# A recurrent attention and a channel mix: value scaling and token differences of the later blocks move from VectorE to GpSimd

## The chip, the cores and the metric

The kernel runs on one core of a Trainium2 chip. The metric is the device time of one execution in microseconds (us), given as the median of several runs. The engines are named as in the profile: PE is TensorE (PEld its weight loads), DVE is VectorE, ACT is ScalarE, POOL is GpSimd, SP is SyncE. SP computes nothing here; it issues DMAs.

## The reference

A retention recurrence over 768 tokens for 4 batches and 8 heads of 64 channels, followed by a channel mix with two projections and a gate. Cut to the core:

```python
# q, k, v: (4, 8, 768, 64)
gamma = 1.0 - 2.0 ** (-5.0 - np.arange(H))
for t in range(S):
    state = gamma[None, :, None, None] * state + einsum('bhd,bhe->bhde', k[:, :, t], v[:, :, t])
    y[:, :, t] = scale * einsum('bhd,bhde->bhe', q[:, :, t], state)
x = y.transpose(0, 2, 1, 3).reshape(B, S, H * D)         # (4, 768, 512)
x_prev = concatenate([zeros, x[:, :-1, :]], axis=1)
xk = mu_k * x + (1.0 - mu_k) * x_prev
xr = mu_r * x + (1.0 - mu_r) * x_prev
k = maximum(xk @ w_k, 0.0)                               # 512 -> 1024
v = k * k @ w_v                                          # 1024 -> 512
out = 1.0 / (1.0 + exp(-(xr @ w_r))) * v
```

## The kernel before

The work is cut into twelve blocks of 256 tokens, three for each batch (block n is third n % 3 of batch n // 3). The recurrence is computed block by block as matmuls of scores, a masked intra-block part and a carried state; the channel mix of a block then uses the block's output, channels on partitions.

The order of all work is written out by hand in one long string, `ORDER` (lines 31 to 82). Each word is a step, its block, and after `~` the engine that runs it or issues its DMA (`p` GpSimd, `s` SyncE, `v` VectorE, `a` ScalarE). After `@` stand PSUM banks. Every engine executes its own steps in the order in which they stand in the string, and a step waits for what it needs; nothing reorders them.

The steps that matter here, with n the block:

- `lv.n`, `lq.n`, `lk.n` (`load`, lines 242 to 261): load values, queries and keys. Most of these are two DMAs each, one for every half of the tokens. Queries and keys are cast to fp16 on the way; values stay fp32. Values, queries and keys have four buffers each, so `lv.10` overwrites the values of block 6 and must wait until `vs.6` has read them.
- `vs.n` (`scale_v`, line 280): multiplies the values of a block (128 x 1024, fp32) with powers of gamma and writes fp16. Three buffers.
- `tq.n`, `tk.n` (line 351): for blocks 9, 10 and 11 alone, the queries and keys are transposed by a DMA on SyncE's queue, in the order tq.10, tk.10, tk.9, tq.9, tq.11, tk.11, with the stores of results (`st`, line 713) between them on the same queue. For the other blocks TensorE transposes (`Tq`, `Tk`).
- `S.n` (line 375): scores of a block on TensorE; `M.n` (line 420): mask, on VectorE.
- `C.n` (line 432 for blocks 6 to 11): the block's state from keys and scaled values, on TensorE. `U`, `G` (lines 485, 494): sum and decay of the state.
- `I.n`, `Y.n` (lines 507, 528): the block's output on TensorE, from the carried state and from the scaled values.
- `D.n` (`yout`, line 573 for blocks 6 to 11): moves the output from PSUM to the tile `xT` with its scale, on VectorE.
- `dx.n` (`differ`, line 595): difference of neighbouring tokens of `xT` (128 x 1024, fp32), for the mix.
- `X.n` (`mixed`, line 621): `dx * mu + x_prev` on VectorE, into `xk` and `xr`.
- `K` (lines 635, 645), `R` (688), `V` (700): the projections on TensorE. `O` (706): the result, on VectorE.

Blocks are grouped for the mix (`GROUPS`, line 19): blocks 6 and 7 form one group and 9 and 10 another, so the mix of block 6 is done with that of block 7.

Of the kernel before, what the change touches and what calls it, by code (L numbers as in the profile page):

```python
# [49 lines left out]
S.5.0@01 O.1.0 O.0.1 lv.5~p lq.6~p M.5.0~v S.5.1@23 vs.5~v K.3.2@5 Qa.3.3 lk.6~p Qb.3.3 K.3.5@4  # L50
M.5.1~v X.2.1.0 Qa.3.2 X.2.1.2 Tq.6@67 Qa.3.5 Tk.6@01 Eq.6~a lv.6~p lv.7~p Ek.6~a C.5@5 U.5.0
X.3.1.0 Qb.3.1 K.3.0@4 Qa.3.0 lk.7~p K.3.7@6 S.6@23 Qb.3.2 M.6~v I.5@01 Y.5 vs.6~v V.2.1.0@7
R.2.1@2 lv.10~p Qb.2.2 Qa.3.7 K.3.4@6 st.0.0 vs.7~v Qb.3.7 s.2.1 st.0.1 V.2.1.1 Tk.7@45 Qb.3.5
Qa.3.4 X.3.1.3 X.3.1.1 Qb.3.0 C.6@23 st.1.0 J.5 Ek.7~a X.3.1.2 R.2.0@6 lv.8~p U.6.0~a D.5~v
U.6.1 U.6.2 U.6.3 V.2.0.0@4 s.2.0 K.3.6@6 dx.5~v Qa.3.6 lq.8~p lk.8~p st.1.1 R.4.1@5 I.6@01
O.2.1 st.2.1 X.5.0.1 s.4.1 G.6~a V.2.0.1 O.2.0 X.5.1.0 X.5.0.3 R.3.1@6 s.3.1 C.7@23 U.7.0 S.7@45
Y.6 M.7~v V.3.1.0@7 X.5.0.2 D.6~v R.4.0@6 lk.9~p Qb.3.4 vs.8~v V.3.0.0@4 R.3.0@5 X.5.1.2 s.4.0
Qb.3.6 V.4.1.0@6 V.3.0.1 V.3.1.1 X.5.1.3 V.4.1.1 U.7.1 U.7.2 X.5.1.1 I.7@01 U.7.3 Tk.8@23 O.3.1
s.3.0 O.3.0 R.5.1@7 Ek.8~a st.3.1 lv.9~p dx.6~v X.5.0.0 s.5.1 C.8@45 Tq.8@23 Y.7 K.5.0@7 O.4.1
vs.9~v st.4.1 Eq.8~a D.7~v K.5.3@6 dx.7~v X.6.0.2 G.7~v Qa.5.0 Qb.5.0 st.2.0 lq.10~p tq.10~s  # L60
K.5.1@7 Qa.5.1 X.6.0.3 X.6.0.1 Qa.5.3 K.5.2@2 Qa.5.2 st.3.0 lk.10~p tk.10~s lv.11~p U.8.0 U.8.1
U.8.2 R.5.0@7 tk.9~s s.5.0 X.6.0.0 V.4.0.0@6 V.4.0.1 O.4.0 Qb.5.1 lk.11~p lq.9~p Qb.5.3
V.5.0.0@7 V.5.1.0@2 S.8@01 M.8~v I.8@45 X.6.1.3 Qb.5.2 V.5.0.1 K.6.4@6 X.6.1.1 O.5.0 Qa.6.4
K.6.7@3 Qa.6.7 K.6.3@6 Qa.6.3 X.6.1.0 lq.11~p X.6.1.2 K.6.1@3 Qa.6.1 Y.8 D.8~v C.9@01 Qb.6.1
vs.10~v U.9.0~a S.10@67 M.10~v U.9.1 dx.8~v X.8.0.3 X.8.0.2 Qb.6.3 K.6.6@3 X.8.0.0 Qb.6.7 Qa.6.6
Qb.6.6 V.5.1.1 K.6.2@4 Qa.6.2 X.8.0.1 Qb.6.2 K.6.5@3 tq.9~s Qa.6.5 R.6.1@4 s.6.1 tq.11~s st.5.0
K.6.0@6 O.5.1 U.9.2 U.9.3 G.9~v R.6.0@7 s.6.0 R.7.1@4 Qb.6.4 s.7.1 st.5.1 K.8.3@7 Qa.8.3 S.9@23
tk.11~s I.9@45 Qa.6.0 Qb.6.0 Qb.6.5 C.10@01 U.10.0 M.9~v R.7.0@7 s.7.0 U.10.1 U.10.2 U.10.3
K.8.2@6 K.8.1@2 Qa.8.1 vs.11~v Qb.8.1 V.6.0.0@7 Y.9 I.10@01 C.11@23 G.10~v V.6.0.1 Qa.8.2
V.7.1.0@6 D.9~v K.8.0@4 Qa.8.0 Qb.8.0 Qb.8.2 U.11.0 U.11.1 U.11.2 V.7.1.1 dx.9~v O.7.1 st.7.1  # L70
Qb.8.3 I.11@23 Y.10 D.10~v dx.10~v X.9.0.0 S.11@45 M.11~v X.9.0.2 V.7.0.0@6 V.7.0.1 V.6.1.0@0
V.6.1.1 V.8.0.0@1 V.8.0.1 X.9.0.1 V.8.1.0@4 V.8.1.1 st.4.0 X.9.0.3 K.9.0@5 O.7.0 K.9.4@6 X.9.1.1
Qa.9.0 Qa.9.4 Qb.9.4 X.9.1.0 O.6.0 st.6.0 Qb.9.0 X.9.1.3 X.8.1.2 Y.11 X.9.1.2 O.6.1 K.9.2@5
Qa.9.2 Qb.9.2 K.9.6@6 Qa.9.6 X.8.1.3 K.9.7@7 Qa.9.7 Qb.9.7 K.9.1@0 Qa.9.1 Qb.9.1 K.9.3@5 Qa.9.3
Qb.9.3 R.10.0@7 R.9.1@0 s.9.1 st.6.1 D.11~v R.9.0@5 s.9.0 st.7.0 X.8.1.1 K.9.5@6 V.10.1.0@5
Qa.9.5 Qb.9.5 Qb.9.6 V.10.0.0@6 X.8.1.0 dx.11~v R.8.1@0 s.8.1 V.9.1.0@2 R.8.0@0 X.11.0.2
X.11.1.3 X.11.0.0 X.11.0.3 X.11.0.1 K.11.1@3 s.8.0 K.11.3@0 Qa.11.3 O.8.0 st.8.0 s.10.0
V.9.0.0@1 Qa.11.1 Qb.11.1 K.11.2@0 Qa.11.2 O.8.1 st.8.1 K.11.0@7 X.11.1.2 V.10.0.1 Qb.11.2
Qb.11.3 V.9.1.1 Qa.11.0 R.10.1@0 Qb.11.0 V.10.1.1 O.9.1 st.9.1 s.10.1 X.11.1.0 X.11.1.1 V.9.0.1
# [794 lines left out]
```

## Time and profile before

| | |
|---|---|
| median of 3 runs | 154.39 us (154.21 to 154.42) |
| span of the profiled execution | 152.4 us, first to last instruction; the profile gives no other time of its own |
| PE busy | 145.3 us (95%) |
| DVE busy | 128.0 us (84%) |
| ACT busy | 94.5 us (62%) |
| POOL busy | 62.1 us (41%), all but four memsets of it DMA issues |
| granted TensorE clock | 1.000 over the whole span |

Times in the profile are counted from the start of the span. A row of a timeline gives the start, the length, the engine, the source line, the operation and tiles, and in brackets the idle time ahead of it and what ended that. In a row of DMA issues the last number is the time from issue to landing.

### The profile page before, as it was taken

The numbers are of one execution on the slowest core, as the hardware profiler recorded it, in microseconds if no ns is written. First come the engines' busy times: TensorE is split into PE (matmuls) and PEld (weight loads), VectorE is DVE, ScalarE is ACT, GpSimd is POOL, SyncE is SP. The second block draws the span as 40 slices with busy tenths as digits, with TensorE's granted clock in tenths as the row PEclk, the third lists the DMA queues.
The fourth block names the chain that finished last, engine by engine and source line by source line (L and its number), as shares of the span: only waits on it lengthen the run. The fifth ranks groups of instructions, "written<-read, shape, count | busy, mean of one in ns | idle before, by whom it ended". The sixth has DMA issues, their size and how long they took to land.

```text
span 152.4 us, 4956 instructions
## 1 busy us (share of the span) xinstructions
PE 145.3 (95%) x2129; PEld 82.4 (54%) x2129; DVE 128.0 (84%) x204; ACT 94.5 (62%) x172; POOL 62.1 (41%) x77
## 2 busy tenths in 40 slices
PE   7969899999999999999999999999999999999991
PEld 3345467657864545545448544447664444466460
DVE  2289999999999999999999998998999999331651
ACT  3655259979955679966418807869450089739430
POOL 7965658999746920599989000000000000000000
PEclk9999999999999999999999999999999999999999
DMA  5999999999999999299999999928103013003153
GB/s 146 237 241 192 181 240 237 148 148 223 167 178 216 213 225 286 68 239 166 258 188 238 236 168 126 152 89 109 38 4 138 0 71 142 0 0 138 69 207 138
DMA packets 56525, 23.83 MB, mean 156 GB/s; under 512 B 48056, under 2 KB 52024, under 8 KB 56504
## 3 DMA queue, kind: packets, MB, share of 16 engines
q0 software_dynamic: 45200, 14.95, 82.1%
q1 hardware_dynamic: 10872, 8.26, 22.3%
q8 instruction: 16, 0.26, 0.7%
q10 hardware_dynamic: 432, 0.32, 0.7%
q14 instruction: 5, 0.04, 0.1%
HBM read 24.31 MB, written 6.29 MB: 201 GB/s over the span
## 4 chain that ended last, share of the span: by engine, by line
PE 73%; DVE 11%; DMA 11%; issue 2%; ACT 0%; DVEq 0%; POOLq 0%
PE ps L700 24%; PE ps L688 14%; PE ps L635 12%; PE ps L645 11%; DMA kT<-k 6%; DMA v<-in_v_dram 5%; DVE a L420 3%; PE ps L507 2%; PE ps L311 2%; DVE xk L621 2%; DVE xT L580 2%; DVE dx L595 2%; PE ps L544 1%; DVE vs L280 1%; PE ps L388 1%
## 5 line engine op out<-in xcount | busy, mean ns | idle before, releaser
L700 PE MATMUL ps<-wv,k2s 128*128 128x512 f16 x184 | 43.9, 380 | 0.0
L667 ACT ACTIVATE kr<-ps 128x512 f32<-128x512 f32 x48 | 27.9, 594 | 23.0 <-PE ps L635 14.9
L700 PEld LDWEIGHTS <-k2s 128*128 128x128 f16 x184 | 17.2, 98 | 19.0
L706 DVE SCALAR_TENSOR_TENSOR os<-ps,rs 128x512 f32<-128x512 f32 x23 | 15.2, 684 | 12.1 <-PE ps L700 6.5
L688 PE MATMUL ps<-wr,xr 128*128 128x512 f16 x96 | 24.0, 379 | 0.0
L259 POOL DMA_DIRECT2D v<-in_v_dram x20 | 18.0, 911 | 13.6 <-DVE vs L280 8.3
L645 PE MATMUL ps<-xk,wk 128*128 128x256 f16 x192 | 23.4, 273 | 0.0
L635 PE MATMUL ps<-xk,wk 128*128 128x512 f16 x96 | 22.8, 379 | 0.0
L420 DVE TENSOR_TENSOR a<-ps,c_sb 128x1024 f16<-128x1024 f32 (+1 forms) x20 | 21.9, 1110 | 0.0
L694 ACT ACTIVATE rs<-ps 128x512 f32<-128x512 f32 x24 | 14.3, 594 | 10.6 <-PE ps L688 8.8
L645 PEld LDWEIGHTS <-wk 128*128 128x128 f16 x192 | 18.2, 98 | 3.9
L621 DVE SCALAR_TENSOR_TENSOR xr<-dx,mu,xT 128x256 f16<-128x256 f32 (+1 forms) x36 | 19.3, 566 | 0.0
L621 DVE SCALAR_TENSOR_TENSOR xk<-dx,mu,xT 128x256 f16<-128x256 f32 (+1 forms) x36 | 18.9, 569 | 0.3
L259 POOL DMA_DIRECT2D k<-in_k_dram x20 | 17.7, 896 | 3.5 <-DMA wv<-in_moe_w_v_dram 1.6
L280 DVE TENSOR_TENSOR vs<-v,csm_sb 128x1024 f16<-128x1024 f32 x12 | 14.5, 1217 | 3.3 <-DMA v<-in_v_dram 3.3
L675 ACT ACTIVATE k2s<-kr 128x512 f16<-128x512 f32 x24 | 14.7, 626 | 0.4
L595 DVE TENSOR_TENSOR dx<-xT 128x1024 f32<-128x1024 f32 x12 | 14.6, 1221 | 0.2
L635 PEld LDWEIGHTS <-wk 128*128 128x128 f16 x96 | 9.1, 98 | 10.5 <-issue 0.2
L679 ACT ACTIVATE k2s<-kr 128x512 f16<-128x512 f32 x24 | 14.5, 625 | 0.3
L688 PEld LDWEIGHTS <-xr 128*128 128x128 f16 x96 | 9.0, 98 | 10.0
L265 ACT COPY qT<-ps 128x1024 f16<-128x1024 f16 (+1 forms) x10 | 9.2, 924 | 7.7 <-PE ps L317 3.7
L265 ACT COPY kT<-ps 128x1024 f16<-128x1024 f16 (+1 forms) x10 | 9.3, 934 | 6.9 <-PE ps L306 3.4
(73 smaller groups left out, 151.3 us busy)
## 6 DMA issues: line engine op xcount, KB each, us to landing
out_dram<-os SPq DMA_DIRECT2D x23, 256.0 KB, 3.8
v<-in_v_dram POOLq DMA_DIRECT2D x20, 256.0 KB, 6.8
k<-in_k_dram POOLq DMA_DIRECT2D x21, 128.0 KB, 6.9
q<-in_q_dram POOLq DMA_DIRECT2D x13, 128.0 KB, 7.1
q<-in_q_dram POOLq DMA_DIRECT2D x5, 256.0 KB, 9.0
v<-in_v_dram POOLq DMA_DIRECT2D x2, 512.0 KB, 7.3
wv<-in_moe_w_v_dram POOLq DMA_DIRECT2D x2, 512.0 KB, 9.5
wk<-in_moe_w_k_dram POOLq DMA_DIRECT2D x2, 256.0 KB, 9.6
```

Of the source, the lines that this page charges most:

```text
L259: e.dma_start(out=to[:, i, hs], in_=src[:, i])
L265: e.copy(out=out, in_=in_)
L280: e.tensor_tensor(out=VS(n), in0=V32(n).rearrange("p (h i d) -> p i h d", i=2, h=H), in1=gks[:, int(half(n) or wide(n)), :, :, None].to_br ...
L420: nc.vector.tensor_tensor(out=dst, in0=dst if n in SPLITM else src, in1=mask[:, None, None, :].to_broadcast(list(dst.shape)), op=ALU.mult,)
L595: e.tensor_tensor(out=DX(k)[:, :, m * TM + t0 : m * TM + t1], in0=x[:, :, c + t0 : c + t1], in1=x[:, :, c - 1 + t0 : c - 1 + t1], op=ALU.s ...
L621: nc.vector.scalar_tensor_tensor(out=XM[w](k)[:, j, t0:t1], in0=DX(k)[:, j, t0:t1], scalar=mu[:, w * NCO + j : w * NCO + j + 1], in1=x[:, ...
L635: nc.tensor.matmul(banks("K", n, g), lhsT=wk16[:, co, g * P : g * P + P], rhs=XM[0](k)[:, co, :], start=(co == 0), stop=(co == NCO - 1),)
L645: nc.tensor.matmul(pz[:, i, :], lhsT=wk16[:, co, fo * P : fo * P + P], rhs=XM[0](k)[:, co, m * TM + t0 : m * TM + t1], start=(i == 0 and c ...
L667: nc.scalar.activation(out=kr, in_=banks("K", n, g, *u), func=AF.Relu)
L688: nc.tensor.matmul(banks("R", n, tb), lhsT=XM[1](k)[:, co, t : t + P], rhs=wr16[:, co, :], start=(co == 0), stop=(co == NCO - 1),)
L700: nc.tensor.matmul(banks("V", n, tb), lhsT=K2(n)[:, fo, tb * P : tb * P + P], rhs=wv16[:, fo, :], start=(fo == 0), stop=(fo == NFO - 1),)
L706: nc.vector.scalar_tensor_tensor(out=OS(2 * n + tb), in0=banks("V", n, tb), scalar=1.0 / (KSC * KSC), in1=RS(2 * n + tb), op0=ALU.mult, op ...
```

## The change

Three things change in `ORDER`, and nothing else in the kernel:

- `vs.8` to `vs.11` and `dx.7` to `dx.11` run on GpSimd, at the same places in the string.
- `lv.8` to `lv.11` are issued by SyncE. `lv.10` stands where it stood; `lv.9` and `lv.11` move forward, to stand right behind `lv.8`.
- With that, `lv.8` to `lv.11` leave GpSimd's queue, and nine arithmetic steps enter it among the loads of queries and keys.

```diff
-R.2.1@2 lv.10~p Qb.2.2 Qa.3.7 K.3.4@6 st.0.0 vs.7~v Qb.3.7 s.2.1 st.0.1 V.2.1.1 Tk.7@45 Qb.3.5
-Qa.3.4 X.3.1.3 X.3.1.1 Qb.3.0 C.6@23 st.1.0 J.5 Ek.7~a X.3.1.2 R.2.0@6 lv.8~p U.6.0~a D.5~v
+R.2.1@2 lv.10~s Qb.2.2 Qa.3.7 K.3.4@6 st.0.0 vs.7~v Qb.3.7 s.2.1 st.0.1 V.2.1.1 Tk.7@45 Qb.3.5
+Qa.3.4 X.3.1.3 X.3.1.1 Qb.3.0 C.6@23 st.1.0 J.5 Ek.7~a X.3.1.2 R.2.0@6 lv.8~s lv.9~s lv.11~s U.6.0~a D.5~v
 U.6.1 U.6.2 U.6.3 V.2.0.0@4 s.2.0 K.3.6@6 dx.5~v Qa.3.6 lq.8~p lk.8~p st.1.1 R.4.1@5 I.6@01
...
-Y.6 M.7~v V.3.1.0@7 X.5.0.2 D.6~v R.4.0@6 lk.9~p Qb.3.4 vs.8~v V.3.0.0@4 R.3.0@5 X.5.1.2 s.4.0
+Y.6 M.7~v V.3.1.0@7 X.5.0.2 D.6~v R.4.0@6 lk.9~p Qb.3.4 vs.8~p V.3.0.0@4 R.3.0@5 X.5.1.2 s.4.0
...
-s.3.0 O.3.0 R.5.1@7 Ek.8~a st.3.1 lv.9~p dx.6~v X.5.0.0 s.5.1 C.8@45 Tq.8@23 Y.7 K.5.0@7 O.4.1
-vs.9~v st.4.1 Eq.8~a D.7~v K.5.3@6 dx.7~v X.6.0.2 G.7~v Qa.5.0 Qb.5.0 st.2.0 lq.10~p tq.10~s
-K.5.1@7 Qa.5.1 X.6.0.3 X.6.0.1 Qa.5.3 K.5.2@2 Qa.5.2 st.3.0 lk.10~p tk.10~s lv.11~p U.8.0 U.8.1
+s.3.0 O.3.0 R.5.1@7 Ek.8~a st.3.1  dx.6~v X.5.0.0 s.5.1 C.8@45 Tq.8@23 Y.7 K.5.0@7 O.4.1
+vs.9~p st.4.1 Eq.8~a D.7~v K.5.3@6 dx.7~p X.6.0.2 G.7~v Qa.5.0 Qb.5.0 st.2.0 lq.10~p tq.10~s
+K.5.1@7 Qa.5.1 X.6.0.3 X.6.0.1 Qa.5.3 K.5.2@2 Qa.5.2 st.3.0 lk.10~p tk.10~s U.8.0 U.8.1
 U.8.2 R.5.0@7 tk.9~s s.5.0 X.6.0.0 V.4.0.0@6 V.4.0.1 O.4.0 Qb.5.1 lk.11~p lq.9~p Qb.5.3
 V.5.0.0@7 V.5.1.0@2 S.8@01 M.8~v I.8@45 X.6.1.3 Qb.5.2 V.5.0.1 K.6.4@6 X.6.1.1 O.5.0 Qa.6.4
 K.6.7@3 Qa.6.7 K.6.3@6 Qa.6.3 X.6.1.0 lq.11~p X.6.1.2 K.6.1@3 Qa.6.1 Y.8 D.8~v C.9@01 Qb.6.1
-vs.10~v U.9.0~a S.10@67 M.10~v U.9.1 dx.8~v X.8.0.3 X.8.0.2 Qb.6.3 K.6.6@3 X.8.0.0 Qb.6.7 Qa.6.6
+vs.10~p U.9.0~a S.10@67 M.10~v U.9.1 dx.8~p X.8.0.3 X.8.0.2 Qb.6.3 K.6.6@3 X.8.0.0 Qb.6.7 Qa.6.6
...
-K.8.2@6 K.8.1@2 Qa.8.1 vs.11~v Qb.8.1 V.6.0.0@7 Y.9 I.10@01 C.11@23 G.10~v V.6.0.1 Qa.8.2
-V.7.1.0@6 D.9~v K.8.0@4 Qa.8.0 Qb.8.0 Qb.8.2 U.11.0 U.11.1 U.11.2 V.7.1.1 dx.9~v O.7.1 st.7.1
-Qb.8.3 I.11@23 Y.10 D.10~v dx.10~v X.9.0.0 S.11@45 M.11~v X.9.0.2 V.7.0.0@6 V.7.0.1 V.6.1.0@0
+K.8.2@6 K.8.1@2 Qa.8.1 vs.11~p Qb.8.1 V.6.0.0@7 Y.9 I.10@01 C.11@23 G.10~v V.6.0.1 Qa.8.2
+V.7.1.0@6 D.9~v K.8.0@4 Qa.8.0 Qb.8.0 Qb.8.2 U.11.0 U.11.1 U.11.2 V.7.1.1 dx.9~p O.7.1 st.7.1
+Qb.8.3 I.11@23 Y.10 D.10~v dx.10~p X.9.0.0 S.11@45 M.11~v X.9.0.2 V.7.0.0@6 V.7.0.1 V.6.1.0@0
...
-Qa.9.5 Qb.9.5 Qb.9.6 V.10.0.0@6 X.8.1.0 dx.11~v R.8.1@0 s.8.1 V.9.1.0@2 R.8.0@0 X.11.0.2
+Qa.9.5 Qb.9.5 Qb.9.6 V.10.0.0@6 X.8.1.0 dx.11~p R.8.1@0 s.8.1 V.9.1.0@2 R.8.0@0 X.11.0.2
```

## The prediction

> **What bounds the kernel now.** I read the page first, then the chain of waits in order of time, then the timelines of TensorE, VectorE, GpSimd's DMA queue and SyncE's queue between 60 and 105 us, where the moved steps lie.
>
> ```profile
> span 152.4 us, 4956 instructions
> ...
> PE 145.3 (95%) x2129; PEld 82.4 (54%) x2129; DVE 128.0 (84%) x204; ACT 94.5 (62%) x172; POOL 62.1 (41%) x77
> ```
>
> TensorE is busy for 95% of the span, so what can be won is small from the start. The windows of 4 us around the changed part say how small (first number the length, then busy time of PE, PEld, DVE, ACT, POOL):
>
> ```profile
> 94.00:98.00 4.00, 3.57 (x124) 2.12 (x124) 3.79 (x6) 3.58 (x7) 0.00 (x0) 1.00 1.38 161
> 98.00:102.00 4.00, 4.00 (x20) 1.83 (x19) 3.96 (x7) 2.48 (x5) 0.00 (x0) 1.00 0.38 99
> ```
>
> Of the thirteen such windows from 62 to 114 us the other twelve have TensorE at 4.00 of 4.00; only the first row here shows a hole, of 0.43 us. VectorE is nearly as full (3.79, 3.96), but TensorE does not wait for it. GpSimd does nothing here, which is what invites the change. The chain (start, length, what) names the hole's cause:
>
> ```profile
> 85.78 0.39 ACT rs L694
> 86.17 9.21 DMA kT<-k
> 95.38 0.04 issue
> 95.42 0.45 PE ps L375 x32
> ```
>
> The DMA transpose of the keys of block 10 (tk.10, line 351, on SyncE's queue) is issued at 86.17 and lands 9.21 us later, and the scores of block 10 (S.10, line 375) start as it lands. So there is a second path with no slack at all: load of q and k of block 10 on GpSimd's queue, transposes on SyncE's queue, S.10. Any delay of tk.10 is a delay of TensorE.
>
> **What is taken from VectorE.** Nine instructions go: vs.8 to vs.11 and dx.7 to dx.11.
>
> ```profile
> L595 DVE TENSOR_TENSOR dx<-xT 128x1024 f32<-128x1024 f32 x12 | 14.6, 1221 | 0.2
> L280 DVE TENSOR_TENSOR vs<-v,csm_sb 128x1024 f16<-128x1024 f32 x12 | 14.5, 1217 | 3.3 <-DMA v<-in_v_dram 3.3
> ...
> L858 POOL MEMSET const-float32-1.0<- 128x1 f32 x1 | 0.1, 99 | 0.0
> ...
> L750 DVE MEMSET warm<- 128x1 f32 x1 | 0.1, 59 | 0.0
> ```
>
> That is 4 x 1.217 + 5 x 1.221 = 11.0 us of VectorE. It lies beside TensorE work, and buys at most the 0.43 us hole, which is a wait for a DMA, so in fact nothing. On GpSimd the trace has no tensor arithmetic. The same work on VectorE, 1.22 us, is my lower bound for one operation; the one kind that both engines run, a 128x1 memset, is 99 ns against 59 ns, a factor of 1.68, which gives 1.22 x 1.68 = 2.05 us; three times VectorE, 3.7 us, is my upper bound. I take the middle one, 2.1 us, as an estimate from these rows. The Trainium skill's page "GPSIMD Engine Reference", section "Elementwise — side-by-side cycle accounting", gives about 2.6 cycles an element at 1.2 GHz for two inputs, for 1024 elements an estimate of 2.2 us, and by that price the sum below would be 0.1 us larger.
>
> **Where the nine land.** GpSimd executes its list in order, and that list also issues the loads. In the built program it now reads: lq.8, lk.8, lk.9, a reload of GpSimd's library (new), vs.8, vs.9, dx.7, then lq.10, lk.10, lk.11, lq.9, lq.11, and behind these vs.10, dx.8, vs.11, dx.9, dx.10, dx.11. Before, the queue ran far ahead:
>
> ```profile
> 62.64 3.53 POOL L259 DMA_DIRECT2D v<-in_v_dram  x4 [8.34 <-DVE vs L280]
> ...
> 72.26 1.85 POOL L259 DMA_DIRECT2D q<-in_q_dram  x2
> 74.15 1.75 POOL L259 DMA_DIRECT2D k<-in_k_dram  x2
> ...
> 80.24 3.53 POOL L259 DMA_DIRECT2D q<-in_q_dram  x4
> ```
>
> The 72.26 row is lq.10, the 74.15 row lk.10, the 80.24 row lq.9 and lq.11. Now all of them stand behind dx.7, which reads xT of block 7 and so waits for yout(7) (D.7) on VectorE, which itself waits for block 7's intra and inter matmuls on TensorE:
>
> ```profile
> 80.15 0.41 PE L432 MATMUL ps<-vs,k 64*64 64x64 f16 x22
> ...
> 80.93 0.35 PE L507 MATMUL ps<-qT,tg 64*64 64x64 f16 x16
> ...
> 94.52 0.47 PE L432 MATMUL ps<-vs,k 64*64 64x64 f16 x32
> 95.42 0.45 PE L375 MATMUL ps<-qT,kT 64*64 64x64 f16 x32 [0.43 <-DMA kT<-k]
> ```
>
> ```profile
> 81.54 1.22 DVE L280 TENSOR_TENSOR vs<-v,csm_sb 128x1024 f16<-128x1024 f32 x1
> 82.67 1.48 DVE L573 TENSOR_TENSOR xT<-ps,gy_sb 128x512 f32<-128x512 f32 x2
> 84.19 1.22 DVE L595 TENSOR_TENSOR dx<-xT 128x1024 f32<-128x1024 f32 x1
> 85.45 0.75 DVE L621 SCALAR_TENSOR_TENSOR xk<-dx,mu,xT 128x512 f16<-128x512 f32 x1
> ```
>
> The 80.93 row ends block 7's matmuls at 81.28. VectorE reached D.7 at 82.67 behind vs.9; without vs.8 and vs.9 it could be there at 82.67 - 2.43 = 80.2, so D.7 now starts with the matmuls' end, about 81.35, and ends 1.48 later, at 82.85. dx.7 on GpSimd: 82.9 to 85.0. So lq.10 goes out at 85.0 in place of 72.26, and even with a GpSimd operation that cost nothing it would be 82.9.
>
> **What hangs on lq.10.** SyncE's queue, also in order:
>
> ```profile
> 82.69 2.51 SPq L351 DMA_TRANSPOSE qT<-q  x1
> 85.26 0.69 SPq L713 DMA_DIRECT2D out_dram<-os  x1
> 86.17 6.99 SPq L351 DMA_TRANSPOSE kT<-k  x2
> 93.26 4.04 SPq L351 DMA_TRANSPOSE qT<-q  x2
> ```
>
> tq.10 at 82.69 reads what lq.10 loads; tk.10 follows 3.48 us behind it (a store between), then tk.9, tq.9 and tq.11. Landing times, from answers for one load each (a v load, the second after the queue had been idle; one of lq.10's own), and the spread over the transposes:
>
> ```profile
> v<-in_v_dram POOLq DMA_DIRECT2D x1, 256.0 KB, 6.1
> ```
>
> ```profile
> q<-in_q_dram POOLq DMA_DIRECT2D x1, 128.0 KB, 7.1
> ```
>
> ```profile
> DMA to landing us min/median/max: 4.3/8.3/9.2
> ```
>
> lq.10 is two DMAs; the second is issued 1.85 / 2 = 0.9 us after the first, at 85.9, into a queue that has been idle, so I take 6.1 us: landed at 92.0 (7.1 would give 93.0). tq.10 at 92.1, tk.10 3.48 later at 95.6; lk.10, out at 86.9 to 88.6, has landed by then. tk.10 lands 9.2 us later, at 104.8: I keep its own duration because the four loads lq.9 and lq.11 are issued just ahead of the transposes now as then (they went out from 80.24, tq.10 at 82.69; now from 90.4 and 92.2). S.10 then starts at 104.8 in place of 95.4: **+9.4 us**. TensorE is in order, so everything behind S.10 moves as a block; it is full afterwards, so nothing is won back. The later transposes move with tk.10, and their users with S.10.
>
> **What I cost at nothing.** vs.8 is needed at 80.15 (the state of block 8). lv.10 now stands on SyncE's queue with its wait for vs.6, which ended in 62.6 (the 62.64 row); behind it st.0.0, st.0.1, st.1.0, then lv.8, lv.9, lv.11. With 0.69 us for a store and, as an estimate, the same for each load DMA, lv.8 is out at 62.7 + 7 x 0.69 = 67.5, landed at 73.6, scaled at 75.7, 4.4 us ahead of its user; vs.9 follows to 77.8, long before 94.52. The cover is gone if one of the seven issues costs over 1.3 us; at the dearest issue of that queue (6.99 / 2 = 3.5) vs.8 would be 15 us late instead, though all rows of plain copies there speak for under 1. The stores held behind the loads have their buffers rewritten by later results, a few us later. The library reload has from lk.9 (issued at about 60) to 73.6, some 13 us; no row shows its length. The same page of the skill (GPSIMD Engine Reference, section "Instruction dispatch") puts a first call after loading at some 6 us, which would fit under that cover. vs.10 and vs.11 run while TensorE stands still; dx.8 too. dx.9 to dx.11 are read by the mixing on VectorE, which now waits 2.1 instead of 1.22 us and has lost 11 us of other work: nothing.
>
> **Sum.** The profiled execution's span is 152.4 us, the runs' median 154.39, so 2.0 us lie around the span. 152.4 + 9.4 + 2.0 = **163.8 us**.
>
> **Rivals.**
> *Transposes run quicker in a quieter DMA system.* At 4.3 us (the quickest of them) tk.10 lands at 99.9, +4.5: 158.9. For it: the last transpose, which ran alone, took this. Against: those that overlapped loads took up to 9.2, and loads overlap again. Chance 0.12.
> *VectorE and GpSimd hold each other up.* vs.8 and vs.9 on GpSimd fall between 73 and 78, where VectorE has no gaps. If each holds VectorE for its 2.1 us, VectorE reaches D.7 at 80.2 + 4.2 = 84.4, 3.1 later than assumed; dx.7, lq.10 and S.10 follow: 166.9, and 168 if an operation takes 3 us. It decides as soon as the hold exceeds 1.1 us. Before shows nothing of it, as GpSimd never computed; the 82.67 and 85.45 rows are the sort of instruction that would be held. The Trainium skill, "SBUF — State Buffer", section "SBUF: two separate sides", states that the two share a port pair as "an exclusive lock, not a bandwidth split", against VectorE instructions with two SBUF inputs where GpSimd reads SBUF; mixing (L621) has two such inputs, D.7 and the masks read PSUM for one, so by that rule only some would be held. Chance 0.20.
> *SyncE's queue jams under the eight new loads.* Over 1.3 us each, vs.8 misses 80.15; at 2 us each it is ready at 62.7 + 14 + 6.1 + 2.1 = 84.9, 4.7 late, and everything above moves by that: 168.5. Chance 0.05.
> *Faster.* If lq.10 did not have to wait (GpSimd's DMA issues passing its arithmetic), it would go out with lk.9 before 62, tk.10 would land early, and the 0.43 us hole would close: 154.0. It decides at lq.10 issued before 82.69 - 7.1 - 0.9 = 74.7. Against: the 62.64 row shows lk.8 and the rest held 8.34 us behind one waiting load, so this queue does keep order, and dx.7 cannot start before 81.3 + 1.5. Chance 0.03. That the change does nothing has no path: 0.01.
>
> **Numbers.** The forecast keeps 0.59, with its own range of 161.5 to 165.5: an operation of 1.2 to 3.7 us (-0.9, +1.6), lq.10 landing in 6.1 or 7.1 (+1.0), tk.10 in the middling 7.5 to 9.2 (down to -1.7). To hold 8 in 10 the range reaches up to the mutual hold and down to the quick transposes: 159 to 168. A measurement tells about 0.2% (0.3 us) from no change; faster 0.03, same 0.01, slower 0.96.
>
> **What would show it.** In the profile of the changed kernel: lq.10 on GpSimd's queue at about 85 instead of 72.26, right behind a GpSimd operation of line 595; tq.10 at about 92; an idle stretch of TensorE of 9 to 10 us ahead of S.10, released by the DMA of kT; no other hole of over 1 us; VectorE waiting for GpSimd ahead of the first mixing of block 6. It would be wrong if lq.10 went out before 75, if TensorE's long hole stood ahead of C.8, or if VectorE's instructions between 70 and 80 stretched.

## The result and the profile after

The changed kernel takes 164.02 us (163.27 to 164.45) against 154.39 us: 6.2% slower, ratio 1.0622, 95% interval 1.0572 to 1.0671. The forecast was 163.8 us, but two of its terms were wrong in opposite directions, as the trace shows. The execution profiled took 163.27 us, so 1.8 us lie around its span. Medians here and below count every execution and ratios leave out those over 1.5% above the fastest of their kernel, so the two can differ by some 0.3%.

The page of the changed kernel, and its windows of 4 us as before (length, then busy time of PE, PEld, DVE, ACT, POOL, granted clock, DMA share, GB/s):

```profile
span 161.5 us, 4961 instructions
...
PE 146.8 (91%) x2129; PEld 82.8 (51%) x2129; DVE 120.4 (75%) x195; ACT 94.4 (58%) x172; POOL 72.1 (45%) x78
```

```profile
94.00:98.00 4.00, 0.95 (x81) 0.79 (x80) 0.52 (x1) 2.53 (x5) 1.54 (x1) 1.00 2.07 195
98.00:102.00 4.00, 0.00 (x0) 0.00 (x0) 2.88 (x5) 0.00 (x0) 0.84 (x1) 0.70 1.92 128
102.00:106.00 4.00, 3.76 (x40) 1.71 (x41) 3.00 (x6) 1.17 (x2) 2.92 (x2) 0.50 0.89 214
106.00:110.00 4.00, 4.00 (x19) 1.75 (x18) 2.26 (x5) 2.35 (x5) 0.00 (x0) 0.95 0.53 127
```

TensorE stands still ahead of S.10 as forecast, though from 95 to 102 us and not to 104.8. What was not forecast stands in the clock column: it falls to 0.50, and in the third window TensorE is busy for nearly the whole time at half speed. GpSimd's and SyncE's queues in order of time:

```profile
71.62 1.90 POOL L280 TENSOR_TENSOR vs<-v,csm_sb 128x1024 f16<-128x1024 f32 x1 [11.89 <-PE ps L528]
74.05 1.90 POOL L280 TENSOR_TENSOR vs<-v,csm_sb 128x1024 f16<-128x1024 f32 x1 [0.53 <-DMA v<-in_v_dram]
82.94 1.89 POOL L595 TENSOR_TENSOR dx<-xT 128x1024 f32<-128x1024 f32 x1 [7.00 <-DVE xT L573]
84.78 1.83 POOL L259 DMA_DIRECT2D q<-in_q_dram  x2
86.60 3.52 POOL L259 DMA_DIRECT2D k<-in_k_dram  x4
90.05 3.55 POOL L259 DMA_DIRECT2D q<-in_q_dram  x4
```

```profile
65.20 7.07 SPq L259 DMA_DIRECT2D v<-in_v_dram  x6
72.31 10.18 SPq L713 DMA_DIRECT2D out_dram<-os  x5
90.04 1.34 SPq L351 DMA_TRANSPOSE qT<-q  x1
91.44 1.23 SPq L713 DMA_DIRECT2D out_dram<-os  x1
92.85 5.40 SPq L351 DMA_TRANSPOSE kT<-k  x2
```

dx.7 waits 7 us for D.7 (released by DVE, line 573); lq.10 goes out right behind it at 84.78, where it was 72.26. tq.10 follows at 90.04 (was 82.69) and tk.10 at 92.85 (was 86.17). The chain of waits and TensorE's rows (block 10's scores, then those of block 9):

```profile
92.85 9.34 DMA kT<-k
102.19 0.04 issue
102.24 0.64 PE ps L375 x26
```

```profile
102.24 0.64 PE L375 MATMUL ps<-qT,kT 64*64 64x64 f16 x32 [7.29 <-DMA kT<-k]
102.81 1.89 PE L635 MATMUL ps<-xk,wk 128*128 128x512 f16 x4
...
112.45 0.45 PE L375 MATMUL ps<-qT,kT 64*64 64x64 f16 x32
```

Four matmuls of line 635 took 1.04 us before, and take 1.89 us right behind the hole. The same step, and the start of S.9, in the kernel before:

```profile
95.80 1.04 PE L635 MATMUL ps<-xk,wk 128*128 128x512 f16 x4
...
103.68 0.45 PE L375 MATMUL ps<-qT,kT 64*64 64x64 f16 x32
```

The 9.1 us that the span grew by, 152.4 to 161.5, come out thus:

| stretch | before | after | difference |
|---|---|---|---|
| to S.10 | 95.42 | 102.24 | +6.8, the late transpose |
| S.10 to S.9 | 8.3 (to 103.68) | 10.2 (to 112.45) | +1.95, the slower clock |
| S.9 to the end | 48.7 | 49.05 | +0.3 |

The last 0.3 us include dx.10. The mixing that feeds K.9 waits 2.07 us for it, where VectorE's own dx took 1.22; the chain passes through it and through the mask of block 11 before it is back on TensorE.

```profile
123.77 1.90 POOL dx L595
```

### The profile page after: what moved, and what is told of

Read it like the earlier page. It is cut to its first block, busy times and chain, and to the rows that moved or that the text cites. A ratio compares the mean times of both kernels' runs of the same rounds, so it can differ in the third digit from the quotient of the medians.

```text
span 161.5 us, 4961 instructions
## 1 busy us (share of the span) xinstructions
PE 146.8 (91%) x2129; PEld 82.8 (51%) x2129; DVE 120.4 (75%) x195; ACT 94.4 (58%) x172; POOL 72.1 (45%) x78
## 4 chain that ended last, share of the span: by engine, by line
PE 63%; DMA 16%; DVE 14%; issue 3%; POOL 2%; SPq 1%; DVEq 0%; POOLq 0%
PE ps L700 20%; PE ps L688 11%; PE ps L635 11%; PE ps L645 10%; DMA k<-in_k_dram 7%; DMA kT<-k 6%; DVE a L420 3%; DMA out_dram<-os 3%; DVE xk L621 2%; PE ps L311 2%; PE ps L507 2%; DVE xT L580 2%; DVE dx L595 1%; DVE vs L280 1%; PE ps L388 1%
## 5 line engine op out<-in xcount | busy, mean ns | idle before, releaser
L700 PE MATMUL ps<-wv,k2s 128*128 128x512 f16 x184 | 44.9, 385 | 0.0
L595 POOL TENSOR_TENSOR dx<-xT 128x1024 f32<-128x1024 f32 x5 | 9.5, 1893 | 41.0 <-DVE xT L573 29.6
L621 DVE SCALAR_TENSOR_TENSOR xk<-dx,mu,xT 128x256 f16<-128x256 f32 (+1 forms) x36 | 19.5, 586 | 6.3 <-POOL dx L595 6.2
L635 PE MATMUL ps<-xk,wk 128*128 128x512 f16 x96 | 23.9, 391 | 0.0
L621 DVE SCALAR_TENSOR_TENSOR xr<-dx,mu,xT 128x256 f16<-128x256 f32 (+1 forms) x36 | 21.1, 616 | 0.0
L280 POOL TENSOR_TENSOR vs<-v,csm_sb 128x1024 f16<-128x1024 f32 x4 | 7.7, 1925 | 12.4 <-PE ps L528 11.9
L485 DVE TENSOR_TENSOR tg<-ps,tg 128x256 f16<-128x256 f32 x20 | 8.4, 419 | 5.2 <-PE ps L432 4.9
```

The lines of the kernel that those rows point to most:

```text
L621: nc.vector.scalar_tensor_tensor(out=XM[w](k)[:, j, t0:t1], in0=DX(k)[:, j, t0:t1], scalar=mu[:, w * NCO + j : w * NCO + j + 1], in1=x[:, ...
L635: nc.tensor.matmul(banks("K", n, g), lhsT=wk16[:, co, g * P : g * P + P], rhs=XM[0](k)[:, co, :], start=(co == 0), stop=(co == NCO - 1),)
L700: nc.tensor.matmul(banks("V", n, tb), lhsT=K2(n)[:, fo, tb * P : tb * P + P], rhs=wv16[:, fo, :], start=(fo == 0), stop=(fo == NFO - 1),)
```

## The experiments

Ratios are against the kernel before, timed beside each (154.05 us for e1 to e8, 153.96 us for e9 to e11).

| kernel | us | ratio, 95% interval |
|---|---|---|
| e1, only dx.7 on GpSimd | 165.5 | 1.0715 [1.0655, 1.0774] |
| e2, the change with dx.7 on VectorE | 156.28 | 1.0154 [1.0104, 1.0205] |
| e3, the change with four loads ahead of vs.8 | 162.99 | 1.0572 [1.0532, 1.0612] |
| e4, the change with the hole filled | 162.16 | 1.0511 [1.0458, 1.0564] |
| e5, only the value loads on SyncE | 162.36 | 1.0571 [1.0527, 1.0614] |
| e6, six late operations on GpSimd | 155.04 | 1.0070 [1.0046, 1.0093] |
| e7, lv.10 further back | 154.36 | 1.0017 [0.9995, 1.0040] |
| e8, all nine on GpSimd, loads reordered | 160.64 | 1.0394 [1.0352, 1.0437] |
| e9, e6 without vs.10 | 154.89 | 1.0059 [1.0035, 1.0083] |
| e10, the change with four loads behind vs.8 | 155.66 | 1.0128 [1.0087, 1.0168] |
| e11, e10 with vs.10 on VectorE | 154.48 | 1.0010 [0.9978, 1.0041] |

**e1: one step of the change alone.**

```diff
 # before
-dx.7~v
+dx.7~p
```

> The kernel before with one step moved: dx.7 on GpSimd, all else on VectorE and in its old queue. My theory (the loads lq.10, lk.10 stand behind dx.7 in GpSimd's list, so the transposes for block 10 and then S.10 come late, and TensorE's clock falls in the hole): D.7 ends at 84.15 here as VectorE still runs vs.8 and vs.9, dx.7 to 86.0, tk.10 lands as in the changed kernel some 17.4 us after lq.10 goes out, at 103.5, S.10 8 us late, and 2 us of slower clock behind it: 164.5 us (163 to 166). Rival (the cost is VectorE and GpSimd holding each other up, about equally in the nine operations): a ninth of 9.6 us, 155.5. Rival (the value loads on SyncE's queue cost it): 154.4, no change.

165.5 us. This one step costs at least as much as the whole change (the two intervals overlap a little). dx.7 starts at 83.68, lq.10 goes out at 85.52, tk.10 takes 11.76 us, and S.10 starts at 104.67, 9.25 us late:

```profile
104.67 0.64 PE L375 MATMUL ps<-qT,kT 64*64 64x64 f16 x32 [9.63 <-DMA kT<-k]
```

**e2: that step undone in the change.**

```diff
 # after
-dx.7~p
+dx.7~v
```

> The changed kernel with dx.7 back on VectorE; the other eight operations stay on GpSimd and the value loads on SyncE. My theory: lq.10 goes out behind vs.9 at about 76 and lands at 82, as tq.10's turn comes on SyncE's queue, so nearly all of the loss is gone: 154.4 us (154.0 to 155.5), TensorE's longest hole under 1 us and the clock at 1.0 throughout. Rival (mutual holds): eight ninths of the loss stay, about 163. Rival (SyncE's queue jammed by the value loads): 164, unchanged.

156.28 us: some 7.4 of the 9.6 us come back, and the clock stays at 1.0, so dx.7's place is most of the cost. The 2.2 us that stay are above what I expected: S.10 still starts 1.7 us later than in the kernel before, behind a hole of 1.37 us. lq.9 and lq.11 now go out at 80.90 to 84.45, just ahead of tk.10, which takes 10.55 us:

```profile
86.55 10.55 DMA kT<-k
```

**e3: the order of the loads changed, all else as in the change.**

```diff
 # after
-lk.9~p Qb.3.4 vs.8~p ... lq.10~p tq.10~s ... lk.10~p tk.10~s ... lq.9~p ... lq.11~p
+lk.9~p lq.10~p lk.10~p lq.9~p lq.11~p Qb.3.4 vs.8~p ... tq.10~s ... tk.10~s
```

> The changed kernel with the same nine operations on GpSimd, but lq.10, lk.10, lq.9 and lq.11 moved in GpSimd's list from behind dx.7 to ahead of vs.8. My theory: they go out between 60 and 70, the transposes go out when SyncE's stores let them (82 to 83), and nothing of the loss is left: 154.0 us (153.6 to 154.8); if tk.10 lands sooner, as the loads no longer run beside it, the old hole of 0.43 us ahead of S.10 closes too. Rival (mutual holds): 164, unchanged, as all nine operations are still there. Rival (GpSimd's slower arithmetic on the path of the mixing): some 1 to 2 us stay.

162.99 us: my expectation was wrong by 9 us. The hole ahead of S.10 is gone, but two others stand earlier, ahead of S.7 and of R.5:

```profile
72.95 0.45 PE L375 MATMUL ps<-qT,kT 64*64 64x64 f16 x32 [2.73 <-DVE os L706]
...
84.55 1.09 PE L688 MATMUL ps<-wr,xr 128*128 128x512 f16 x4 [3.21 <-DVE os L706]
```

Both are released by VectorE's results (line 706), which wait for a store to free their buffer. On SyncE's queue the six loads of lv.8, lv.9 and lv.11 take 12.46 us here, against 7.07 in the change, and the stores stand behind them:

```profile
67.55 12.46 SPq L259 DMA_DIRECT2D v<-in_v_dram  x6
80.06 8.23 SPq L713 DMA_DIRECT2D out_dram<-os  x5
```

So e3 put the four loads beside the value loads. Whether that or GpSimd's arithmetic cost the time, e5 and e10 tell apart.

**e5: the value loads moved, no arithmetic.**

```diff
 # before
-lv.10~p ... lv.8~p ... lv.9~p ... lv.11~p
+lv.10~s ... lv.8~s lv.9~s lv.11~s
```

> The kernel before with only the value loads lv.8 to lv.11 moved to SyncE, as in the change; all nine operations stay on VectorE. GpSimd's queue is then not held by lv.10 and sends lq.10, lk.10, lq.9 and lq.11 between 59 and 75, as in e3, beside the value loads. Theory drawn from e3 (stores stand behind value loads on SyncE, the loads of both queues slow each other, VectorE's results wait for the stores' buffers, and TensorE for VectorE): holes ahead of S.7 and of R.5 as in e3, 6 us in all: 160 us (157 to 162), with no arithmetic on GpSimd at all. Rival (what e3 lost came from GpSimd's arithmetic or the library reload): 154.0, or a little faster as the loads run ahead.

162.36 us, just above the range that I gave, with nothing but DMA issues on GpSimd. The same two holes, of 2.10 and 2.38 us, have the same releaser; VectorE's results waited 2.68 and 4.16 us for stores:

```profile
85.30 1.29 DVE L706 SCALAR_TENSOR_TENSOR os<-ps,rs 128x512 f32<-128x512 f32 x2 [4.16 <-DMA out_dram<-os]
```

Moving the value loads to SyncE is thus harmful when nothing else is moved. How the stores come late shows on SyncE's queue. Its first three stores go out from 63.00, behind lv.10, which stands there until vs.6 has read its buffer; in the kernel before the queue's stores start at 54.92. The fourth goes out at 76.24, behind six value loads (before 69.84).

```profile
63.00 6.09 SPq L713 DMA_DIRECT2D out_dram<-os  x3
```

The first of the two holes is followed by a stretch at the 0.50 clock, from about 74 to 77.5 us, which is part of the loss. In the whole change nearly all of this was spared (0.16 us ahead of S.7): vs.8, which starts at 71.62, and dx.7 behind it kept the loads of q and k away from the value loads. In e2 vs.8 and vs.9 did that without dx.7: lq.10 goes out at 75.63, and neither hole is there.

**e10 and e11: the loads placed behind vs.8, when the value loads have been issued.**

```diff
 # after
-lk.9~p Qb.3.4 vs.8~p ... lq.10~p tq.10~s ... lk.10~p tk.10~s ... lq.9~p ... lq.11~p
+lk.9~p Qb.3.4 vs.8~p lq.10~p lk.10~p lq.9~p lq.11~p ... tq.10~s ... tk.10~s
 # e11 also
-vs.10~p
+vs.10~v
```

> The changed kernel with all nine operations on GpSimd and the value loads on SyncE as in the change; only lq.10, lk.10, lq.9 and lq.11 are moved in GpSimd's list, from behind dx.7 to between vs.8 and vs.9, so they go out from 73.5 on, when the value loads have ended. My theory, without what confounded e3: tq.10 goes at 82 to 83, tk.10 lands by about 95.5, no hole there and no drop of the clock; vs.10 now falls at 86.6 beside VectorE's mixing and holds it, about 1 us as in e6: 155.0 us (154.3 to 156), so 9 of the 9.6 us come back. Rival (nine operations on GpSimd or SyncE's value loads cost by themselves): 160 or more, as e3, e5 and e8.

> As e10, with vs.10 back on VectorE. Theory (what e10 keeps is the hold by vs.10): 154.1 us (153.7 to 154.8). Rival (something else keeps it): as e10.

155.66 and 154.48 us. All nine operations and the SyncE loads are as in the change in e10; four loads stand elsewhere, and about 8 of the 9.6 us are gone: the queue's order is the cause. What is left in e10 is a hole ahead of I.8, and VectorE's rows show where it comes from:

```profile
85.09 3.29 DVE L494 TENSOR_TENSOR tg<-t,csm_sb 128x256 f16<-128x256 f32 x1
```

```profile
86.15 1.94 POOL L280 TENSOR_TENSOR vs<-v,csm_sb 128x1024 f16<-128x1024 f32 x1
```

```profile
90.55 0.19 PE L507 MATMUL ps<-qT,tg 64*64 64x64 f16 x1 [1.40 <-DVE tg L485]
```

The decay of the state takes 0.42 us in the kernel before and 3.29 us here, ending at 88.38, just behind GpSimd's vs.10 (88.09). With vs.10 back on VectorE, e11 is level with the kernel before. It has a hole of 1.52 us ahead of K.5, since vs.9, now at 79.58, holds a mixing for 2.23 us, while the old 0.43 us hole is closed.

**e4: the hole filled.**

```diff
 # after
-U.9.0~a S.10@67
+U.9.0~a z.28@6 S.10@67
```

> The changed kernel with seven fp32 matmuls of zeros (about 0.87 us each, 6.1 us in all, as the warm-up ones at the start) put ahead of S.10 on TensorE, into the bank that S.10 then overwrites: TensorE works where it stood still. Theory (the granted clock falls after the hole, which costs 2.0 us of the 9.0): S.10 starts at 102.2 as before, the clock stays at 1.0, and the time falls by about 2 us to 162. Rival (what follows S.10 is slow because VectorE and ScalarE had run dry or wait for GpSimd): 164, unchanged.

162.16 us, as expected. S.10 starts at 102.07, practically as in the change, the clock is 1.0 throughout, and S.10 to S.9 is back at 8.26 us:

```profile
102.07 0.45 PE L375 MATMUL ps<-qT,kT 64*64 64x64 f16 x32 [1.32 <-DMA kT<-k]
...
110.33 0.45 PE L375 MATMUL ps<-qT,kT 64*64 64x64 f16 x32
```

**e6 and e9: GpSimd's arithmetic behind all loads.**

```diff
 # before; e9 leaves vs.10 on VectorE
-vs.10~v ... dx.8~v ... vs.11~v ... dx.9~v ... dx.10~v ... dx.11~v
+vs.10~p ... dx.8~p ... vs.11~p ... dx.9~p ... dx.10~p ... dx.11~p
```

> The kernel before with only vs.10, vs.11 and dx.8 to dx.11 on GpSimd, behind all loads; vs.8, vs.9, dx.7 and every load stay as they were. Theory (GpSimd's arithmetic costs nothing where no load stands behind it): no change, 154.0 us (153.7 to 154.6), VectorE freed of 7.3 us that TensorE does not need. Rival (mutual holds of VectorE and GpSimd, or the 0.7 us longer dx of blocks 9 and 10 on the path to K.9): 0.5 to 2 us slower.

> As e6, but vs.10 stays on VectorE: only vs.11 and dx.8 to dx.11 are on GpSimd. Theory from e6 (GpSimd's vs.10 held VectorE's dx.7, an operation with two inputs in SBUF, 1.5 us, and that made the 0.9 us hole on TensorE ahead of I.8): the hole goes, 154.1 us, no change (153.7 to 154.5). Rival (the later dx cost it): 155.0 as e6.

155.04 us: the rival of e6 holds. VectorE's dx.7, 1.22 us in the kernel before, takes 2.71 us beside vs.10 on GpSimd, and TensorE waits 0.60 and 0.27 us ahead of I.8:

```profile
83.81 2.71 DVE L595 TENSOR_TENSOR dx<-xT 128x1024 f32<-128x1024 f32 x1
```

```profile
83.48 1.96 POOL L280 TENSOR_TENSOR vs<-v,csm_sb 128x1024 f16<-128x1024 f32 x1
```

dx.7 ends at 86.52, 1.1 us behind vs.10's end at 85.44: it stood until GpSimd had finished, then ran. In e9 that hole is gone, as expected, but the time is 154.89 us, not 154.1. Its profile has 1.04 us ahead of S.10 (before 0.43), because tk.10 went out 0.3 us later and again took 9.3; the issues ahead of it on SyncE's queue took longer, and why is open. But S.10 starts only 0.37 us later than before, and the span grew by some 1.0. The rest comes behind S.10, where the chain of waits runs through dx.8 on GpSimd (2.80 us here, beside VectorE's vs.10) and four mixings behind it, the first of which took 2.11 us beside vs.11 (all four took 1.67 us before):

```profile
100.10 3.30 DVE L621 SCALAR_TENSOR_TENSOR xk<-dx,mu,xT 128x256 f16<-128x256 f32 x4 [0.32 <-POOL dx L595]
```

So e9's rival, that the later dx cost it, is right for a part; how large a part was not tested.

**e7 and e8: the queue freed.**

```diff
 # before, e7
-lv.10~p Qb.2.2 ... lv.9~p
+Qb.2.2 ... lv.9~p lv.10~p
 # e8: all nine on GpSimd, and
+lk.9~p lv.9~p lv.10~p lq.10~p lk.10~p Qb.3.4 vs.8~p lv.11~p lq.9~p lq.11~p
```

> The kernel before with one load moved: lv.10 behind lv.9 in GpSimd's queue, so the queue no longer stands for 8.3 us waiting for vs.6. Nothing is on another engine. Theory (tk.10's landing is slowed by lq.9 and lq.11 running beside it, and that is the 0.43 us hole ahead of S.10): the loads end some 8 us sooner, the transposes land in 5 to 7 us, the hole goes: 153.6 us (153.4 to 154.0). Rival (the hole is the transposes' own time): 154.0, no change.

> All nine operations on GpSimd as in the change, but the value loads on GpSimd's queue and the list ordered so that no load which is needed soon stands behind a waiting operation: lv.8, lq.8, lk.8, lk.9, lv.9, lv.10, lq.10, lk.10, vs.8, lv.11, lq.9, lq.11, vs.9, dx.7, lk.11, vs.10 and the rest. Theory (the loss is the order of the queues alone): 154.0 us (153.6 to 154.8); vs.8 must be done by 80.1, which fails if the reload of the library takes over 8 us. Rival (mutual holds and the slower GpSimd operations cost by themselves): 156 or more.

e7: 154.36 us, not told from the kernel before and above the 153.6 that I expected. The 0.43 us hole did go, as tk.10 landed in 4.38 us, but TensorE has a new one of 1.01 us ahead of line 507 at 65.56, put down to "issue"; e5 (0.88) and e8 (1.43) have it too, e3 has not. It stands inside one step, between matmuls that wait for no semaphore. The DMA queue that the page calls "instruction" (q8) moved 16 KB at 63.2 to 64.1 us in e7 and ended at 63.8 and 64.3 in e5 and e8, but at 62.0 in the kernel before and 61.7 in e3. TensorE may thus have stood for its next instructions; no run tests that, so the cause is open.

e8: 160.64 us, my expectation was wrong by 6.6. The loads come in time, but vs.8 starts at 69.34, beside VectorE's dx.6:

```profile
68.67 3.70 DVE L595 TENSOR_TENSOR dx<-xT 128x1024 f32<-128x1024 f32 x1
```

It ends 2.5 us late, the result behind it (line 706) frees a bank late, and TensorE waits 1.82 us ahead of S.7; vs.10 holds the decay as in e10 (1.40 and 0.27 us); with the 1.43 us and the slow clock behind the S.7 hole (0.50 from 75 to 78) that makes up the loss. No version here beats the kernel before.

## Why the prediction was right, and where it was off

- **GpSimd's order puts lq.10 behind dx.7, behind D.7:** right, and shown to be the cause by e1 (this step alone: +11.5 us), e2 and e10. D.7 ran from 81.39 to 82.87 (forecast 81.35 to 82.85), an operation took 1.89 us (2.1 taken; 2.2 by the second price in the prediction), lq.10 went out at 84.78 (85.0).
- **lq.10 to S.10: too long by 2.3 us.** I took 6.1 us for the landing; the two DMAs landed in 3.8 and 4.2 us (first two rows below), so tq.10 went out at 90.04, not 92.1. The row of the kernel before for the first load after idle (third row) would have been nearer, as GpSimd had sent no load since 59.7 and the value loads had ended. tk.10 followed 2.81 us behind tq.10, not 3.48. tk.10's 9.34 us was as taken (9.2). S.10 moved by 6.8, not 9.4.

```profile
q<-in_q_dram POOLq DMA_DIRECT2D x1, 128.0 KB, 3.8
```

```profile
q<-in_q_dram POOLq DMA_DIRECT2D x1, 128.0 KB, 4.2
```

```profile
v<-in_v_dram POOLq DMA_DIRECT2D x1, 256.0 KB, 3.7
```

- **"TensorE is full afterwards, so everything moves as a block": wrong by 2 us.** The profile of before has the clock at 1.000 throughout, so nothing there showed what a long hole does. e4 prices it: filled, the next stretch is 1.95 us shorter. The Trainium skill, "TensorE: Matmul & The Clock Gate", section "Part 1: The HAM clock gate", says that the clock is halved after an idle window of about 3.4 us and given back after as long a busy one. The after trace agrees (0.50 from about 99.6, 4.6 us into the hole, until about 106.4, 4.2 us behind its end); that sentence would have pointed to the missing term. It does not cover all of this case: in e8 and e5 the clock fell after holes of 1.82 and 2.10 us. The two misses, -2.6 and +2, cancelled by luck, which is why 163.8 met 164.02.
- **"dx.9 to dx.11 cost nothing":** dx.10 is on the chain; it is part of the 0.3 us behind S.9.
- **Mutual hold as a rival:** real, though not what made this change slow. In the change it stretched a mixing to 1.91 us and others by 0.2 to 0.6, where VectorE had time. Two of these lie at 72.91 and 75.11, so the sign that the prediction gave for being wrong, VectorE's instructions stretching between 70 and 80, did come; it cost nothing, as D.7 still started at 81.39. In e6, e8 and e10 the hold reached TensorE. It strikes as the Trainium skill's "SBUF — State Buffer", section "Who interferes with whom", says: two inputs in SBUF are held (dx, mixing, decay), while the sums of line 485, with one input in PSUM, never exceed 0.43 us in any run.
- **SyncE's queue as a rival:** I gave it 0.05 and priced it by issue time alone. In the change it cost 0.16 us ahead of S.7, with 1.18 us for a load (7.07 / 6) and not 0.69; e5 shows 8.3 us when the other queue's loads run beside. Its harm is to the stores queued behind the loads.
- **The library reload under its cover:** right; vs.8 ran from 71.62 to 73.52. In e8 vs.8 starts 0.07 us behind the DMA issue ahead of it, reload between them, so the 6 us quoted beside that term do not show here.
- **Two sums among the rivals do not come out.** At 3 us an operation the mutual hold gives about 169.5, not 168: D.7 starts at 86.2, 4.9 us late, and dx.7 takes 0.9 more. And the cover of vs.8 goes if each of the seven issues costs over 1.3 us, not one of them. The forecast does not use either.

## What to carry to other kernels

Before moving a step to an engine that looks idle, list what that engine still has to issue behind the step: a wait there is a wait for every load behind it, and here one such wait cost as much as the whole change. Check also which stores stand behind moved loads, and what runs on VectorE with both inputs in SBUF at that time. Add to every forecast hole of some microseconds on TensorE the slower stretch that follows it.

## What was not expected of the hardware

- A hole of 1.82 us on TensorE, in e8, was enough for the clock to fall to 0.50 for 3.4 us (rows below); in the change a hole of 7.29 us was followed by 0.50 until 4.2 us behind its end. Length alone does not decide: in e3 the clock stayed at 1.00 behind a hole of 2.73 us, and fell behind one of 3.21.

```profile
74.02 0.45 PE L375 MATMUL ps<-qT,kT 64*64 64x64 f16 x32 [1.82 <-DVE os L706]
```

```profile
75.00:76.00 1.00, 1.00 (x3) 0.36 (x4) 1.00 (x2) 0.64 (x2) 1.00 (x2) 0.50 1.04 318
```

- VectorE is held from before GpSimd's recorded start: in e10 the decay starts at 85.09, vs.10 at 86.15, with a load being issued ahead of vs.10. In the change the mixing of 1.91 us ran from 90.85 to 92.75 and was over before vs.10's recorded start at 93.54, while GpSimd's rows show loads being issued; in the kernel before, where GpSimd issues loads and computes nothing, no such instruction is stretched. The Trainium skill ("GPSIMD Engine Reference", section "Instruction dispatch") says that a core of GpSimd begins its share of the next instruction as soon as it has finished its own, which would fit; no run here shows the single cores.
- DMA transposes of one form landed in 3.1 us (tk.11 in the change) to 11.76 us (tk.10 in e1). tk.10 alone took 4.38 us in e7, where the loads of lq.9 and lq.11 had landed before it, and 11.76 in e1, where they ran beside it.
